# Relative-position bias features computed once per distance, mirrored by TensorE and skewed by the store

## The chip, the cores and the metric

The kernel runs on one core of one Trainium2 chip. The metric is the device time of one execution in microseconds. The kernel before takes 676.85 us, the median of three runs (676.49 to 677.21).

## The reference

Attention with a learned relative-position bias (4 batches, 8 heads, 576 positions, head size 64), followed by a two-layer network on the 2304 tokens. Cut to what matters here:

```
pos = np.arange(S)                                   # S = 576
rel = (pos[:, None] - pos[None, :]).astype(np.float32)
psi_rel = np.log1p(np.abs(rel))
psi_i = np.log1p(np.maximum(pos[:, None], 1.0))
x = (psi_rel / psi_i)[..., None]
h = np.maximum(x @ w1 + b1, 0.0)                     # 32 hidden units
bias = h @ w2                                        # one value per head
scores = scale * q @ k.T + bias.transpose(2, 0, 1)   # then softmax, then @ v
...
h = x @ w_in; r = np.maximum(h, 0.0); g = s * (r * r) + b; out = g @ w_out
```

`psi_i` depends on the row alone and is positive, so `relu(w1*L/psi_i + b1)` is `max(w1*L, -b1*psi_i) / psi_i` up to an added constant, with `L = log1p(|i-j|)`. For one row, everything that depends on the column is a function of `|i-j|`.

## The kernel before, in words

The program writes every engine's order by hand (`tc.manual_schedule()`), so the order of the calls in the source is the order on each engine and on the DMA queue of SyncE (SP). It has three parts.

The bias part builds `bias_d` in DRAM, 8 heads x 576 rows x 576 columns, in 36 steps of 16 rows. The 128 partitions are 4 rows x 32 hidden units; a step has four features, `c` = 0 to 3, one for each group of four rows. A feature `f` (`feature`, L114) is `max(ls, thr)` over 576 columns: `ls` holds `w1*log1p(|g + (S-4) - u|)` for the four rows g of the partitions and 1148 offsets u, and a feature reads the 576 of them that belong to its rows. It is made by VectorE (L121), GpSimd (L123) or ScalarE (L125, as a Relu with another constant, `kc` column 1). Which engine makes which feature stands in the strings of L119 (`vvpa`, `vppa`, `vpvp` in turn) and `ends` (L112). `f` is written as 9 blocks of 64 with a pitch of 68.

`bias_step` (L131) multiplies the four features by the block matrix `w2bd` on TensorE, four 32-column groups of the array side by side, 512 columns (L140) and then 64 (L143), in fp32. A PSUM tile `bps` of one step is emptied by one ScalarE instruction (L147) into `stg`, 128 partitions (16 rows x 8 heads) x 576. One DMA on SP stores it (L153). There are 16 buffers of `f` (four steps) and 10 of `stg`. Features are issued two steps ahead of their matmuls (L619). The last four steps also copy head 0 into `be` of the first pair (`first_head`, L156), and the stores of steps 32 to 34 are held back until step 35.

The attention part works on 16 pairs (a head and two batches), five units of 128 rows each, in the calls `scores`, `biased`, `expo`, `probs_t` and `av`; `bt` holds the bias of rows 0 to 511 of a head and `be` that of its last 64 rows, both read from `bias_d`. GpSimd splits q and k into two parts (`split_qk`, L199 and L200). The first score units stand in `plan` (L605) behind bias steps 33 and 34; the loads of `bt` for the first pair stand behind steps 11, 17, 26 and 33. The network part follows, the last 60% of the time.

Of the kernel before, what the change touches and what calls it, by code (L numbers as in the profile page):

```python
# [26 lines left out]
def attention_moe(ctx, tc, q, k, v, w_in, w_out, dist, par, out):  # L27
# [6 lines left out]
    HALF = S // 2  # L34
    NU = dist.shape[1]
    STEPS = S // 16
# [24 lines left out]

    bias_d = dram.tile([H, S, S], F32, name="bias")
    rs_d = [dram.tile([2, S], F32, name=f"rs{p}") for p in range(NP)]
# [8 lines left out]
    warm = const.tile([128, 1], F32, name="warm")  # L72
    dst = dp.tile([128, NU], F32, name="dst")
    pt_ = dp.tile([128, par.shape[1]], F32, name="pt_")
# [5 lines left out]
    w2x = dp.tile([128, 4, 4 * H], F32, name="w2x")  # L80
    ls = dp.tile([128, NU], F32, name="ls")
    thr = dp.tile([128, 4 * STEPS], F32, name="thr")
# [3 lines left out]
    def setup():  # L86
        hi = S - 64
        nc.sync.dma_start(out=pt_, in_=par)
        nc.scalar.dma_start(out=dst[:, hi:], in_=dist[:, hi:])
        nc.sync.dma_start(out=dst[:, 0:hi], in_=dist[:, 0:hi])  # L90
        nc.vector.memset(warm, 0.0)
        nc.scalar.activation(warm, warm, AF.Exp)
        make_identity(nc, ident)
        wps = ps_t.tile([128, 512], F32, tag="t", name="wps")
        for _ in range(8):
            nc.tensor.matmul(wps[:, 0:128], ident, ident, start=True, stop=True)
        nc.vector.tensor_scalar(thr, li, b1c, -1.0, op0=ALU.mult, op1=ALU.mult)
        nc.vector.tensor_copy(w2x, w2bd.unsqueeze(1).broadcast_to([128, 4, 4 * H]))
        nc.vector.tensor_scalar(off, li, b1c, None, op0=ALU.mult)
        nc.vector.tensor_scalar(ls[:, hi:], dst[:, hi:], w1c, None, op0=ALU.mult)  # L100
        nc.scalar.activation(ls[:, 0:hi], dst[:, 0:hi], AF.Copy, scale=w1c)

# [8 lines left out]
    feats, late = {}, []  # L111
    ends = {STEPS - 4: "vvvp", STEPS - 3: "vvva", STEPS - 2: "vpva", STEPS - 1: "vpva"}  # L112

    def feature(st, c):  # L114
        w = NU - S - 16 * st - 4 * c
        f = fp.tile([128, S // 64, 68], F32, tag="f", name="f")[:, :, 0:64]
        src = ls[:, w:w + S].rearrange("p (a b) -> p a b", b=64)
        col = slice(4 * st + c, 4 * st + c + 1)
        kind = (ends.get(st) or ("vvpa", "vppa", "vpvp")[st % 3])[c]  # L119
        if kind == "v":  # L120
            nc.vector.tensor_scalar(f, src, thr[:, col], None, op0=ALU.max)  # L121
        elif kind == "p":
            nc.gpsimd.tensor_scalar(f, src, FLT_MAX, thr[:, col], op0=ALU.min, op1=ALU.max)  # L123
        else:
            nc.scalar.activation(f, src, AF.Relu, bias=off[:, col])  # L125
        return f, kind == "a"

    def bias_features(st):
        feats[st] = [feature(st, c) for c in (2, 0, 3, 1)]

    def bias_step(st):  # L131
# [6 lines left out]
        pb = ps.rearrange("p a b -> p (a b)")  # L138
        for c in range(4):
            nc.tensor.matmul(  # L140
                pb[32 * c:32 * c + 32, 0:512], w2bd, fs[c][0][:, 0:8], start=True, stop=True)
        for c in range(4):
            nc.tensor.matmul(  # L143
                pb[32 * c:32 * c + 32, 512:S], w2bd, fs[c][0][:, 8:9], start=True, stop=True)
        kcol = kc[:, 1:2] if fs[3][1] else kc[:, 0:1]
        stg = fp.tile([128, S], F32, tag="stg", name="stg", bufs=10)
        nc.scalar.activation(stg, pb[:, 0:S], AF.Identity, scale=nr[:, st:st + 1], bias=kcol)  # L147
        if st >= STEPS - 4:
            first_head(st, stg)
        late.append((st, stg))  # L150
        if st < STEPS - 4 or st == STEPS - 1:
            for i, t in late:
                nc.sync.dma_start(out=bias_d[:, 16 * i:16 * i + 16, :].rearrange("h r j -> r h j"), in_=t)  # L153
            late.clear()

    def first_head(st, stg):  # L156
        r0 = 16 * st % 64
        for x in range(2):
            nc.sync.dma_start(out=bes[0][64 * x + r0:64 * x + r0 + 16, :], in_=stg[0:128:H, :])

# [3 lines left out]
    def load_bias(p, t0, t1):  # L164
# [3 lines left out]
        bt = bts[p]  # L168
        rows = bias_d[h, 128 * t0:128 * t1, :].rearrange("(t p) j -> p t j", p=128)
        nc.sync.dma_start(out=bt[:, t0:t1, 64:], in_=rows)  # L170
        nc.sync.dma_start(out=bt[:, t0:t1, 0:64], in_=rows[:, :, 512:S])

    def load_be(p):
        if p == 0:
            bes[0] = io.tile([128, S], F32, tag="be", name="be", bufs=2)
        elif p < NP and pairs[p][0] == pairs[p - 1][0]:
            bes[p] = bes[p - 1]
        elif p < NP:
            bes[p] = io.tile([128, S], F32, tag="be", name="be", bufs=2)
            for x in range(2):  # L180
                nc.sync.dma_start(out=bes[p][64 * x:64 * x + 64, :], in_=bias_d[pairs[p][0], 512:S, :])

# [411 lines left out]
    def fill():  # L594
# [13 lines left out]
        17: ((load_bias, 0, 1, 2),),  # L608
        20: ((load_v, 0), (load_be, 0)),
        28: ((split_qk, 0, 0),),  # L610
# [165 lines left out]
```

## Time and profile before

| | us |
|---|---|
| three runs, median | 676.85 |
| the profiled execution's own time | 676.67 |
| its span, first to last instruction | 674.5 |
| PE busy in the span | 660.2 (98%) |
| VectorE, ScalarE, GpSimd busy | 449.7, 353.5, 181.2 |

PE is TensorE's matmuls, DVE is VectorE, ACT is ScalarE, POOL is GpSimd, SP is SyncE; a `q` behind an engine's name is its queue, which issues DMAs. The granted clock of TensorE is 1.00 in all slices of the page. A share of busy time over the whole span says little here, because the parts have different limits: it has to be read by stage.

### The profile page before, as it was taken

To read this page: it belongs to the slowest core of one execution; us is meant where nothing else is said; L and a number is where in the kernel's file an instruction comes from. 1 tells how busy PE (TensorE), PEld (TensorE's weight loads), DVE (VectorE), ACT (ScalarE), POOL (GpSimd) and SP (SyncE) were. 2 spreads that over 40 slices of the span, in tenths; PEclk is the share of its full clock that TensorE was granted. 3 is DMA by queue.
4 is the path that set the end of the run, shared out by engine and by line. 5 is a ranking of instruction groups with operands and counts; after the bars stand their busy time and mean duration, and the time that the engine had idled before them with its cause. 6 is when DMAs were issued, how large, how long until landed. Compare 5 with 4: busy or idle time off the path is not lost.

```text
span 674.5 us, 13622 instructions
## 1 busy us (share of the span) xinstructions
PE 660.2 (98%) x5202; PEld 506.4 (75%) x5202; DVE 449.7 (67%) x883; ACT 353.5 (52%) x741; POOL 181.2 (27%) x190
## 2 busy tenths in 40 slices
PE   8997999999999999999999999999999999999997
PEld 4445666776677766688888888888888888888886
DVE  7997898898999877458665356655365754443243
ACT  6997877787777777345543333332333322222221
POOL 7995243453354320012121012220022210000000
PEclk9999999999999999999999999999999999999999
DMA  5997676665766452497628345217335223323312
GB/s 159 285 297 238 193 239 212 206 205 181 239 200 204 145 186 67 122 325 262 214 99 311 127 160 196 81 32 262 128 141 187 64 83 150 121 85 141 109 62 94
DMA packets 53648, 114.84 MB, mean 170 GB/s; under 512 B 10576, under 2 KB 18000, under 8 KB 53584
## 3 DMA queue, kind: packets, MB, share of 16 engines
q1 hardware_dynamic: 53440, 113.65, 50.6%
q8 instruction: 41, 0.67, 0.4%
q10 hardware_dynamic: 144, 0.33, 0.2%
q14 instruction: 23, 0.19, 0.1%
HBM read 84.09 MB, written 29.56 MB: 168 GB/s over the span
## 4 chain that ended last, share of the span: by engine, by line
PE 90%; POOL 3%; DVE 2%; ACT 2%; issue 1%; DMA 1%; SPq 0%; POOLq 0%; DVEq 0%; ACTq 0%
PE hps L472 29%; PE o L497 29%; PE xps L355 10%; PE sps L224 10%; PE tps L288 7%; POOL f L123 3%; PE xps L358 3%; PE bps L140 2%; ACT pr L249 1%; DVE tt L238 1%; DMA pt__123<-in_par_dram 1%; DVE f L121 0%; PE xps L288 0%; DMA bias<-stg 0%; ACT stg L147 0%
## 5 line engine op out<-in xcount | busy, mean ns | idle before, releaser
L497 PE MATMUL o<-wh,gt 128*128 128x512 f32 x576 | 190.3, 390 | 0.0
L472 PE MATMUL hps<-x,wh 128*128 128x512 f32 (+1 forms) x640 | 181.7, 368 | 0.0
L476 ACT ACTIVATE r<-hps 128x512 f32<-128x512 f32 (+1 forms) x80 | 44.5, 556 | 211.5 <-PE hps L472 208.5
L477 DVE SCALAR_TENSOR_TENSOR r<-r,sb 128x512 f32<-128x512 f32 (+1 forms) x80 | 56.9, 711 | 144.2 <-ACT r L476 144.1
L249 ACT ACTIVATE pr<-tt,mn 128x576 f32<-128x576 f32 x144 | 110.9, 771 | 46.5 <-DVE mn L238 45.7
L472 PEld LDWEIGHTS hps<-x,wh 128*128 128x128 f32 x640 | 116.9, 188 | 22.0 <-ACT x L452 0.4
L497 PEld LDWEIGHTS o<-wh,gt 128*128 128x128 f32 x576 | 108.2, 188 | 22.6 <-issue 0.3
L472 PE MATMUL hps<-x,wl 128*128 128x512 f32 (+1 forms) x320 | 117.7, 368 | 0.0
L497 PE MATMUL o<-wl,gt 128*128 128x512 f32 x288 | 112.3, 390 | 0.0
L238 DVE CUSTOM_DVE_ANT_0 tt<-sps,bt 128x576 f32<-128x576 f32 x128 | 91.2, 750 | 7.6 <-PE sps L224 6.0
L224 PE MATMUL sps<-kr,qr 64*128 64x288 f32 (+1 forms) x864 | 87.1, 307 | 1.2 <-ACT stg L147 0.9
L482 DVE SCALAR_TENSOR_TENSOR gt<-r,sb,gt 128x512 fp32r<-128x512 f32 (+1 forms) x80 | 62.6, 783 | 38.3 <-ACT gt L481 38.3
L422 POOL TENSOR_TENSOR wl<-full,wh 128x512 fp32r<-128x512 f32 x32 | 43.3, 1354 | 163.7 <-ACT wh L417 137.9
L481 ACT ACTIVATE gt<-r,sb 128x512 fp32r<-128x512 f32 (+1 forms) x80 | 54.5, 681 | 46.9 <-DVE r L477 46.8
L355 PE MATMUL xps<-pt,vt 128*64 128x288 f32 x512 | 76.0, 419 | 1.7 <-DVE rb L363 0.9
L224 PEld LDWEIGHTS sps<-kr,qr 64*128 64x128 f32 (+1 forms) x864 | 69.2, 186 | 3.5 <-ACT stg L147 1.1
L288 PEld LDWEIGHTS tps<-ident,pr 64*128 64x128 f32 x1216 | 43.9, 137 | 35.5 <-issue 28.4
L472 PEld LDWEIGHTS hps<-x,wl 128*128 128x128 f32 x320 | 60.3, 188 | 10.0
L398 POOL TENSOR_SCALAR full<-full 128x512 f32<-128x512 f32 x32 | 23.8, 742 | 152.4 <-ACT full L396 152.2
L497 PEld LDWEIGHTS o<-wl,gt 128*128 128x128 f32 x288 | 54.1, 188 | 10.4
L288 PE MATMUL tps<-ident,pr 64*128 64x64 f32 x1216 | 55.5, 229 | 2.4 <-ACT pt L319 2.1
L321 DVE COPY pt<-tps 128x512 f32<-128x512 f32 x64 | 43.9, 686 | 12.4 <-PE tps L288 12.3
(66 smaller groups left out, 698.4 us busy)
## 6 DMA issues: line engine op xcount, KB each, us to landing
x<-xs SPq DMA_DIRECT2D x48, 512.0 KB
bias<-stg SPq DMA_DIRECT2D x36, 288.0 KB
raw<-in_moe_w_in_dram SPq DMA_DIRECT2D x16, 512.0 KB
raw<-in_moe_w_out_dram SPq DMA_DIRECT2D x16, 512.0 KB
xs<-x SPq DMA_DIRECT2D x16, 512.0 KB
bt<-bias SPq DMA_DIRECT2D x7, 1152.0 KB
qt<-in_q_dram SPq DMA_DIRECT2D x16, 320.0 KB
kt<-in_k_dram SPq DMA_DIRECT2D x16, 320.0 KB
```

Source lines behind the costliest of these rows:

```text
L224: nc.tensor.matmul(o, a, b, start=(i == 0), stop=(i == 2))
L238: nc.vector.tensor_tensor_reduce(tt.rearrange("p (a b) -> p a b", a=2), ps[x][:, :, 0:HALF], bias.rearrange("p (a b) -> p a b", a=2), -1.0 ...
L249: nc.scalar.activation(pr[:, x], tts.pop((n, x)), AF.Exp, bias=mn[:, x:x + 1], scale=-1.0, accum_out=sums[p][:, col // 3, col % 3:col % 3 ...
L288: nc.tensor.matmul(outs[r], src[d], ident[d, d], is_transpose=True, start=start, stop=True, skip_group_check=not start)
L321: nc.vector.tensor_copy(o, i)
L355: nc.tensor.matmul(ps[64 * x:64 * x + 64, hf, 0:HALF], vt[:, 4 * x + kb, :], pt[:, kb, x, c], start=(kb == 0), stop=False)
L472: nc.tensor.matmul(ps[:, 0:n], w[0, g][:, a, fc], xs_t[s, a][:, j, 0:n], start=(i == 0), stop=(i == 3 * KB - 1))
L476: nc.scalar.activation(r, ps[:, 0:n], AF.Relu)
L477: nc.vector.scalar_tensor_tensor(r, r, sb[:, 0:1], r, op0=ALU.mult, op1=ALU.mult)
L481: nc.scalar.activation(hi, r, AF.Identity, bias=sb[:, 1:2])
L482: nc.vector.scalar_tensor_tensor(lo, r, sb[:, 1:2], hi.bitcast(F32), op0=ALU.add, op1=ALU.subtract)
L497: nc.tensor.matmul(o, gt[:, a, tok], w[1, g][:, fo], start=(fo == 0 and j == 0), stop=(fo == 3 and j == 2))
```

## The change

Everything about a feature now depends on the distance `|i-j|` alone. The host's table `dist` becomes `log1p` of 0, 1, 2, ... in blocks of 16 with a pitch of 20 floats, the same in every partition. A feature of step `st` covers the distances 0 to `16*nb - 1` with `nb = max(S-16*st, 16*st+16)/16` blocks: 576 at both ends of the run, 304 in the middle. GpSimd and ScalarE read a table `ls` without gaps, already multiplied by `w1`; VectorE reads `dst` with its gaps, multiplies by `w1` and takes the maximum in one instruction, over an odd number of blocks. All write `f` without gaps.

TensorE mirrors: PSUM column `a` of a step stands for distance `|a - m|`, `m = 16*st + 15`, over S + 15 = 591 columns; columns below `m` read the feature backwards (step -1), the others forwards. With the cut at 512 columns, which the kernel before has too, this makes three matmuls for each `c` in place of two. Row r of a step needs the 576 columns that start at 15 - r: the store shifts each row by one column (`skewed`), into rows of pitch 608, and `bt` and `be` are read from column 16 on. The engine of a feature comes from running sums (`busy`) in place of the strings. The last 64 rows of head 0 go through a small table in DRAM, `tail_d`, stored by four DMAs and read back by two (`load_be(0)`).

```diff
     HALF = S // 2
-    NU = dist.shape[1]
+    NG16 = dist.shape[1] // 20
     STEPS = S // 16
...
-    bias_d = dram.tile([H, S, S], F32, name="bias")
+    PITCH = S + 32
+    bias_d = dram.tile([H, S, PITCH], F32, name="bias")
+    tail_d = dram.tile([64, PITCH], F32, name="btail")
     rs_d = [dram.tile([2, S], F32, name=f"rs{p}") for p in range(NP)]
...
     warm = const.tile([128, 1], F32, name="warm")
-    dst = dp.tile([128, NU], F32, name="dst")
+    dst = dp.tile([128, NG16, 20], F32, name="dst")
     pt_ = dp.tile([128, par.shape[1]], F32, name="pt_")
...
     w2x = dp.tile([128, 4, 4 * H], F32, name="w2x")
-    ls = dp.tile([128, NU], F32, name="ls")
+    ls = dp.tile([128, 16 * NG16], F32, name="ls")
     thr = dp.tile([128, 4 * STEPS], F32, name="thr")
...
     def setup():
-        hi = S - 64
+        flat = dst.rearrange("p a b -> p (a b)")
+        hi = 20 * (NG16 // 2)
         nc.sync.dma_start(out=pt_, in_=par)
-        nc.scalar.dma_start(out=dst[:, hi:], in_=dist[:, hi:])
-        nc.sync.dma_start(out=dst[:, 0:hi], in_=dist[:, 0:hi])
+        nc.scalar.dma_start(out=flat[:, 0:hi], in_=dist[:, 0:hi])
+        nc.sync.dma_start(out=flat[:, hi:], in_=dist[:, hi:])
         nc.vector.memset(warm, 0.0)
...
         nc.vector.tensor_scalar(off, li, b1c, None, op0=ALU.mult)
-        nc.vector.tensor_scalar(ls[:, hi:], dst[:, hi:], w1c, None, op0=ALU.mult)
-        nc.scalar.activation(ls[:, 0:hi], dst[:, 0:hi], AF.Copy, scale=w1c)
+        k = NG16 // 2
+        nc.vector.tensor_scalar(ls[:, 0:16 * k], dst[:, 0:k, 0:16], w1c, None, op0=ALU.mult)
+        nc.scalar.activation(ls[:, 16 * k:], dst[:, k:, 0:16], AF.Copy, scale=w1c)
...
     feats, late = {}, []
-    ends = {STEPS - 4: "vvvp", STEPS - 3: "vvva", STEPS - 2: "vpva", STEPS - 1: "vpva"}
+    busy = {"v": 0.0, "p": 0.0, "a": 0.0}
...
     def feature(st, c):
-        w = NU - S - 16 * st - 4 * c
-        f = fp.tile([128, S // 64, 68], F32, tag="f", name="f")[:, :, 0:64]
-        src = ls[:, w:w + S].rearrange("p (a b) -> p a b", b=64)
+        nb = max(S - 16 * st, 16 * st + 16) // 16
+        kind = min("vpa" if c == 3 else "vp", key=lambda e: busy[e])
+        if kind == "v":
+            nb += 1 - nb % 2
+        busy[kind] += 0.2 - 0.05 * (kind == "p") + nb / 60.0
+        f = fp.tile([128, 16 * NG16], F32, tag="f", name="f")
+        o, src = f[:, 0:16 * nb], ls[:, 0:16 * nb]
         col = slice(4 * st + c, 4 * st + c + 1)
-        kind = (ends.get(st) or ("vvpa", "vppa", "vpvp")[st % 3])[c]
         if kind == "v":
-            nc.vector.tensor_scalar(f, src, thr[:, col], None, op0=ALU.max)
+            nc.vector.tensor_scalar(o, dst[:, 0:nb, 0:16], w1c, thr[:, col], op0=ALU.mult, op1=ALU.max)
         elif kind == "p":
-            nc.gpsimd.tensor_scalar(f, src, FLT_MAX, thr[:, col], op0=ALU.min, op1=ALU.max)
+            nc.gpsimd.tensor_scalar(o, src, FLT_MAX, thr[:, col], op0=ALU.min, op1=ALU.max)
         else:
-            nc.scalar.activation(f, src, AF.Relu, bias=off[:, col])
+            nc.scalar.activation(o, src, AF.Relu, bias=off[:, col])
         return f, kind == "a"
...
         feats[st] = [feature(st, c) for c in (2, 0, 3, 1)]
+        busy["a"] += 0.83
+        busy["p"] += 2.3 * (st in (26, 28))
...
         pb = ps.rearrange("p a b -> p (a b)")
-        for c in range(4):
-            nc.tensor.matmul(
-                pb[32 * c:32 * c + 32, 0:512], w2bd, fs[c][0][:, 0:8], start=True, stop=True)
-        for c in range(4):
-            nc.tensor.matmul(
-                pb[32 * c:32 * c + 32, 512:S], w2bd, fs[c][0][:, 8:9], start=True, stop=True)
+        m = 16 * st + 15
+        cuts = sorted((0, m, 512, S + 15))
+        for a, b in zip(cuts, cuts[1:]):
+            for c in range(4):
+                mov = fs[c][0][:, m - a:m - b:-1] if b <= m else fs[c][0][:, a - m:b - m]
+                nc.tensor.matmul(pb[32 * c:32 * c + 32, a:b], w2bd, mov, start=True, stop=True)
         kcol = kc[:, 1:2] if fs[3][1] else kc[:, 0:1]
-        stg = fp.tile([128, S], F32, tag="stg", name="stg", bufs=10)
-        nc.scalar.activation(stg, pb[:, 0:S], AF.Identity, scale=nr[:, st:st + 1], bias=kcol)
+        stg = fp.tile([128, S + 16], F32, tag="stg", name="stg", bufs=10)[:, 0:S + 15]
+        nc.scalar.activation(stg, pb[:, 0:S + 15], AF.Identity, scale=nr[:, st:st + 1], bias=kcol)
         if st >= STEPS - 4:
-            first_head(st, stg)
+            r0 = 16 * st - (S - 64)
+            nc.sync.dma_start(out=skewed(tail_d[r0:r0 + 16, :]), in_=stg[0:128:H, :])
+        if st == STEPS - 1:
+            load_be(0)
         late.append((st, stg))
...
             for i, t in late:
-                nc.sync.dma_start(out=bias_d[:, 16 * i:16 * i + 16, :].rearrange("h r j -> r h j"), in_=t)
+                nc.sync.dma_start(out=skewed(bias_d[:, 16 * i:16 * i + 16, :]), in_=t)
             late.clear()
...
-    def first_head(st, stg):
-        r0 = 16 * st % 64
-        for x in range(2):
-            nc.sync.dma_start(out=bes[0][64 * x + r0:64 * x + r0 + 16, :], in_=stg[0:128:H, :])
+    def skewed(rows):
+        heads = [[S * PITCH, H]] if len(rows.shape) == 3 else []
+        return bass.AP(rows.tensor, rows.offset + 1, [[PITCH + 1, 16]] + heads + [[1, S + 15]])
...
         bt = bts[p]
-        rows = bias_d[h, 128 * t0:128 * t1, :].rearrange("(t p) j -> p t j", p=128)
+        rows = bias_d[h, 128 * t0:128 * t1, 16:16 + S].rearrange("(t p) j -> p t j", p=128)
         nc.sync.dma_start(out=bt[:, t0:t1, 64:], in_=rows)
...
     def load_be(p):
-        if p == 0:
-            bes[0] = io.tile([128, S], F32, tag="be", name="be", bufs=2)
-        elif p < NP and pairs[p][0] == pairs[p - 1][0]:
+        if 0 < p < NP and pairs[p][0] == pairs[p - 1][0]:
             bes[p] = bes[p - 1]
...
             for x in range(2):
-                nc.sync.dma_start(out=bes[p][64 * x:64 * x + 64, :], in_=bias_d[pairs[p][0], 512:S, :])
+                rows = tail_d if p == 0 else bias_d[pairs[p][0], 512:S, :]
+                nc.sync.dma_start(out=bes[p][64 * x:64 * x + 64, :], in_=rows[:, 16:16 + S])
...
         17: ((load_bias, 0, 1, 2),),
-        20: ((load_v, 0), (load_be, 0)),
+        20: ((load_v, 0),),
         28: ((split_qk, 0, 0),),
...
     nb, nh, S, D = q.shape
-    g = np.arange(4)
-    u = np.arange(2 * S - 4)
-    dist = np.log1p(np.abs(g[:, None] + (S - 4) - u[None, :]).astype(np.float32))
+    nblk = S // 16 // 2 * 2 + 1
+    dist = np.zeros((nblk, 20), np.float32)
+    dist[:, 0:16] = np.log1p(np.arange(16 * nblk, dtype=np.float32)).reshape(nblk, 16)
     logi = np.log1p(np.maximum(np.arange(S, dtype=np.float32), 1.0)).astype(np.float32)
...
         arrays[n] = np.ascontiguousarray(inputs[n]).view(np.int64)
-    arrays['dist'] = np.repeat(dist.astype(np.float32), hid, axis=0)
+    arrays['dist'] = np.repeat(dist.reshape(1, -1), 4 * hid, axis=0)
     arrays['par'] = par
```

How the instructions move, from the two programs as built (counts behind an `x` are equal neighbours).

GpSimd around the splits of the first pair's q and k (`qr`, `kr`), up to the splits of the second pair. Before:

```order
L123 TENSOR_SCALAR f<-ls,thr 128x9x64 x51
L199 TENSOR_SCALAR qr<-qt 128x640
L200 TENSOR_TENSOR qr<-qt,qr 128x640
L123 TENSOR_SCALAR f<-ls,thr 128x9x64 x3
L199 TENSOR_SCALAR kr<-kt 128x640
L200 TENSOR_TENSOR kr<-kt,kr 128x640
L123 TENSOR_SCALAR f<-ls,thr 128x9x64 x2
L199 TENSOR_SCALAR qr<-qt 128x640
```

After, the same place:

```order
L130 TENSOR_SCALAR f<-ls,thr 128x496 x2
L209 TENSOR_SCALAR qr<-qt 128x640
L210 TENSOR_TENSOR qr<-qt,qr 128x640
L130 TENSOR_SCALAR f<-ls,thr 128x512
L130 TENSOR_SCALAR f<-ls,thr 128x528 x2
L209 TENSOR_SCALAR kr<-kt 128x640
L210 TENSOR_TENSOR kr<-kt,kr 128x640
L130 TENSOR_SCALAR f<-ls,thr 128x544 x2
L130 TENSOR_SCALAR f<-ls,thr 128x560
L130 TENSOR_SCALAR f<-ls,thr 128x576 x3
L209 TENSOR_SCALAR qr<-qt 128x640
```

GpSimd has 63 features now (56 before), of 304 to 576 columns, 27440 in all; of these 59 (25152 columns) belong to steps 0 to 33. Six stand behind the split of `kr`, two before.

TensorE at the first two steps (`bps` is the PSUM tile of a step). Before:

```order
L105 MATMUL cps<-pt__123,w2x 128x1
L140 MATMUL bps<-f,pt__123 32x512 x4
L143 MATMUL bps<-f,pt__123 32x64 x4
L140 MATMUL bps<-f,pt__123 32x512 x4
L143 MATMUL bps<-f,pt__123 32x64 x4
```

After, the same two steps:

```order
L109 MATMUL cps<-pt__124,w2x 128x1
L153 MATMUL bps<-f,pt__124 32x15 x4
L153 MATMUL bps<-f,pt__124 32x497 x4
L153 MATMUL bps<-f,pt__124 32x79 x4
L153 MATMUL bps<-f,pt__124 32x31 x4
L153 MATMUL bps<-f,pt__124 32x481 x4
L153 MATMUL bps<-f,pt__124 32x79 x4
```

A step has 12 matmuls over 591 columns in place of 8 over 576; the trace shows each fp32 matmul as two, so 24 and 16.

SP behind step 31's store, up to the first weight loads (`raw`). Before:

```order
L159 DMA be<-stg 16x576 x4
L170 DMA bt<-bias 128x576
L171 DMA bt<-bias 128x64
L187 DMA qt<-in_q_dram 128x640
L193 DMA kt<-in_k_dram 128x640
L207 DMA vt<-in_v_dram 128x640
L159 DMA be<-stg 16x576 x4
L153 DMA bias<-stg 16x8x576 x4
L384 DMA raw<-in_moe_w_in_dram 128x1024 x2
```

After, the same place (`btail` is `tail_d`):

```order
L159 DMA btail<-stg 16x591 x2
L181 DMA bt<-bias 128x576
L182 DMA bt<-bias 128x64
L197 DMA qt<-in_q_dram 128x640
L203 DMA kt<-in_k_dram 128x640
L217 DMA vt<-in_v_dram 128x640
L159 DMA btail<-stg 16x591 x2
L191 DMA be<-btail 64x576 x2
L165 DMA bias<-stg 16x8x591 x4
L394 DMA raw<-in_moe_w_in_dram 128x1024 x2
```

Eight copies of `be` from SBUF become four stores to DRAM and two loads; the loads read what the stores wrote, and the four held-back stores of the bias stand behind them in the queue.

## Rows read from the trace of the kernel before

**Rows 1.** Busy time by stage: stretch and length; engines' busy us (instructions); clock, DMA, GB/s

```profile
10.00:50.00 40.00, 38.31 (x512) 17.46 (x512) 40.00 (x56) 38.38 (x54) 39.47 (x53) 1.00 0.90 274
50.00:70.00 20.00, 15.68 (x225) 11.54 (x221) 15.46 (x40) 15.94 (x38) 10.10 (x10) 1.00 0.83 257
70.00:270.00 200.00, 199.17 (x2565) 140.48 (x2561) 173.95 (x457) 155.88 (x408) 74.66 (x68) 1.00 0.60 187
```

**Rows 2.** Groups by line and shape, 0 to 85 us: busy, mean ns | idle before

```profile
L121 DVE TENSOR_SCALAR f<-ls,thr 128x576 f32<-128x576 f32 x63 | 45.5, 793 | 0.0
...
L123 POOL TENSOR_SCALAR f<-ls,thr 128x576 f32<-128x576 f32 x56 | 40.3, 748 | 4.5 <-DVE ls L100 4.3
L147 ACT ACTIVATE stg<-bps,kc,pt__123 128x576 f32<-128x576 f32 x36 | 29.7, 826 | 3.3 <-PE bps L143 1.9 <-ACT f L125 1.0 <-ACT pr L249 0.4
L125 ACT ACTIVATE f<-ls,off 128x576 f32<-128x576 f32 x25 | 19.1, 766 | 0.0
...
L100 DVE TENSOR_SCALAR ls<-dst,pt__123 128x636 f32<-128x636 f32 x1 | 0.5, 545 | 0.0
```

**Rows 3.** Timeline, 28.5 to 33 us, VectorE, GpSimd, ScalarE: start us, us, instruction, count

```profile
27.89 5.83 DVE L121 TENSOR_SCALAR f<-ls,thr 128x576 f32<-128x576 f32 x8
...
27.88 5.79 POOL L123 TENSOR_SCALAR f<-ls,thr 128x576 f32<-128x576 f32 x8
...
27.90 0.77 ACT L125 ACTIVATE f<-ls,off 128x576 f32<-128x576 f32 x1
28.57 0.83 ACT L147 ACTIVATE stg<-bps,kc,pt__123 128x576 f32<-128x576 f32 x1
29.28 0.77 ACT L125 ACTIVATE f<-ls,off 128x576 f32<-128x576 f32 x1
```

**Rows 4.** Timeline of TensorE, 28 to 29.4 us, one step and the next's start

```profile
28.11 1.07 PE L140 MATMUL bps<-f,pt__123 128*32 128x512 f32 x8
28.97 0.32 PE L143 MATMUL bps<-f,pt__123 128*32 128x64 f32 x8
29.08 0.59 PE L140 MATMUL bps<-f,pt__123 128*32 128x512 f32 x1
```

**Rows 5.** GpSimd's other sizes, 80 to 100 us; then its timeline, 42 to 51 us

```profile
L199 POOL TENSOR_SCALAR kr<-kt 128x640 fp32r<-128x640 f32 x2 | 1.4, 724 | 0.0
...
L398 POOL TENSOR_SCALAR full<-full 128x512 f32<-128x512 f32 x1 | 0.6, 614 | 3.8 <-ACT full L396 3.8
...
47.11 0.72 POOL L199 TENSOR_SCALAR kr<-kt 128x640 fp32r<-128x640 f32 x1
47.92 1.56 POOL L200 TENSOR_TENSOR kr<-kt,kr 128x640 fp32r<-128x640 f32 x1
49.57 1.46 POOL L123 TENSOR_SCALAR f<-ls,thr 128x576 f32<-128x576 f32 x2
```

**Rows 6.** The chain that ended last, 49 to 53 us: start, us, what

```profile
50.55 0.73 ACT stg L147
51.28 0.04 issue
51.32 0.95 PE sps L224 x10
```

**Rows 7.** DMA of 10 to 50 us; then SP's waits, 5 to 44 us (total, times, longest)

```profile
DMA packets 5646, 10.97 MB, mean 274 GB/s; under 512 B 1003, under 2 KB 1003, under 8 KB 5639
...
q1 hardware_dynamic: 5639, 10.88, 88.8%
...
SPq L170 <- DMA bias<-stg: 3.3, 4, 1.0
```

**Rows 8.** Around `be`: timelines of ScalarE, VectorE and SP, with the chain's DMA row

```profile
56.79 0.83 ACT L147 ACTIVATE stg<-bps,kc,pt__123 128x576 f32<-128x576 f32 x1 [0.36 <-ACT pr L249]
...
58.81 2.74 DMA bias<-stg
...
63.16 0.76 DVE L238 CUSTOM_DVE_ANT_0 tt<-sps,be 128x576 f32<-128x576 f32 x1 [0.25 <-issue]
...
82.28 0.25 SPq L271 DMA_DIRECT2D rs<-rt  x1
...
83.03 1.09 SPq L276 DMA_DIRECT2D rb<-rs  x2
```

## The prediction

> **What bounds the kernel now.** I read the busy times by stage first. From 70 us on TensorE is busy 199.17 of 200 us, and the change has no instruction there: what is gained or lost before moves the end one for one. From 10 to 50 us, in the bias part, VectorE is busy all of the time, GpSimd 39.47 and ScalarE 38.38 of 40 us; TensorE shows 38.31, but that counts matmuls that wait in the pipe. From 50 to 70 us nothing is full [rows 1]. Next the groups by line, for counts and lengths [rows 2], and the timeline, for the pace: eight VectorE features in 5.83 us are (5.83 - 0.79)/7 = 0.72 us from start to start, and GpSimd's the same [rows 3]. ScalarE's take 0.67 (27.90 to 28.57) and one `stg` 0.71 (to 29.28). The strings give VectorE and GpSimd five features each in three steps, 3 x 1.2 us = 3.6 us: three engines are balanced at 1.2 us a step. TensorE needs 0.97 for a step that it doesn't wait in (28.11 to 29.08) [rows 4]. Last the chain: `stg` of step 33 ends at 51.28 and the first scores start at 51.32 [rows 6]. So the end of step 33 sets the start of the attention part, and the sum is made for steps 0 to 33.
>
> **The change part by part.** *GpSimd.* Before: 54 features of steps 0 to 33 at 0.72 us and two splits at 2.46 us (47.11 to 49.57), 38.9 + 4.9 = 43.8 us. For shorter features I take the slope from GpSimd's other sizes: 724 ns at 640 columns, 614 at 512, so 0.86 ns a column [rows 5]; of the 0.72 us at 576 columns 0.495 scale and 0.225 stay. After: 59 x 0.225 + 25152 x 0.86 ns = 13.3 + 21.6, and the splits: 39.8 us, 4.0 less. Between the ends: if all of the 0.72 us scaled, because the gaps of `f` cost the rest, 25152 x 1.25 ns + 4.9 = 36.3 us, and if nothing scaled, 59 x 0.72 + 4.9 = 47.4 us. I take 39.8, because two sizes on this engine give the slope.
>
> *VectorE.* 59 features become 60 with 26432 columns. All scaling: 33.0 us; with 0.2 us that stay, 60 x 0.2 + 26432 x 0.9 ns = 35.8 us. Either way it is below GpSimd's 39.8, which covers it, with 0.065 us to spare for each feature, in case a second pointer scalar or the gaps on the reading side cost something. Without that cover each 0.1 us more on a feature would cost 6 us in all, less 4.
>
> *ScalarE.* 23 features become 17, at most 17 x 0.67 = 11.4, and 34 `stg` of 0.71 with 15 more columns (0.02 each) are 24.8: 36.2 us, covered too.
>
> *TensorE.* 0.97 x 591/576 = 0.995 us a step, 33.8 us. The third piece is below 64 columns in a dozen steps; the 64-column piece of before takes 0.11 us (28.97 to 29.08), so this adds at most 1.3 us. Reading backwards stands nowhere in this trace: I take it at the forward rate, since it is the same column stream, with half speed as the other end (a rival below) and no reason for a gain. In steps 11 to 25, where features are shortest, TensorE has 14.9 us and GpSimd 15.4, so there the two wait for each other: nothing if 16 `f` buffers decouple them, 15 x 0.21 = 3.2 us if each step waits out the drain by which the 1.07 us of a matmul group exceed the 0.86 to its next group. I allow 1.0 us, a chosen value nearer to the low end because the ring is four steps deep.
>
> *Stores.* 88.8% of 40 us on 16 DMA engines, 568 us, went to some 4640 long rows (5639 packets less 1003 small ones) [rows 7]: 0.1225 us a row, 0.98 us a store on each engine (8 rows), 30.4 us for 31 stores, and 5.1 us for loads. For 34 steps that is 38.4 us in 40.8; after, with 2364 bytes for 2304, 39.3 us in some 38. The lag of 1.3 us is hidden by ten `stg` buffers, 11 us deep; SP waited only 3.3 us in four waits for such a store to land. If that cover goes, each us of lag costs one.
>
> *Start and end.* `ls` is made in two halves of 288 and 304 columns in place of 636 and 512. That saves VectorE some 0.25 us, but GpSimd now needs both halves: nothing. Four GpSimd features stand behind those of step 33 in place of two, 2.9 us, and `stg` of step 35 comes 6.2 us after that of step 33 (56.79 against 50.55) [rows 6, 8]: hidden.
>
> *`be` through DRAM.* Before, eight copies landed directly. Now the two loads wait on SP for the last tail store to land, and behind them stand the four held-back stores and the weight loads, whose readers come after 70 us. From the end of `stg` 35 (57.62) to the first use (63.16) are 5.54 us [rows 8]. The new path: one issue 0.55 (half of 1.09), landing, two issues 1.09, landing. A small store landed within 0.75 us (82.28 to 83.03), a large one in 2.74: 3.1 to 7.1 us in sum, so a stall of 0 to 1.6 us. The middle, 5.1, is hidden; I put 0.2.
>
> Sum: -4.0 + 1.0 + 0.2 = -2.8 us against the profiled execution's 676.67 (span 674.5 and 2.2 around it), 673.9. The median of the runs stands 0.2 above that execution: 674.1 us.
>
> **Rivals.** *A: the gain is eaten* (chance 0.20). Not GpSimd but its alternation with TensorE decides (2 us and more of the 3.2), and the round trip of `be` stalls VectorE by up to 1.6 in a stretch where everything hangs on it: about 676.3 us. For it: 14.9 against 15.4. Against: TensorE waits little in the trace although it shares its features with three engines.
>
> *B: TensorE becomes the bound* (0.12), slower than before. A step has 24 matmuls in the trace's count in place of 16. If each costs what it costs in the 0.97 us step, 0.061 us, a step is 1.46 us, 49.6 us for 34, 5.8 more than GpSimd's 43.8 of before: 682.8 us with the stall. Half speed for backward columns, about half of 591, gives the same 1.46. It decides from 43.8/34/24 = 0.054 us a matmul. For it: no stage in the rows runs denser than 512 in 40 us or 2565 in 200. Against: nine matmuls start within 28.97 to 29.08, 0.014 us apart [rows 4], and 0.97 is matched by columns as well.
> [...]
>
> *C: the skewed rows are slow to write* (0.07). Rows now start at any multiple of 4 bytes. With 1.5 times the time of a row, 34 x 1.51 + 5.1 = 56.4 us against 38: 18.4 of lag, 11 of them taken by the ring, 7.4 over: 681.5 us. It decides from 1.37 times. For it: the DMA share of 0.90 leaves no room. Against: nothing in the rows shows an odd start costing anything, nor that it is free.
> [...]
>
> *D: VectorE shuts GpSimd out* (0.04). `ls` with 636 columns took 545 ns where a feature of 576 took 793 [rows 2]: VectorE has a faster form. If the features ran in it and kept GpSimd off meanwhile, 26432 x 545/636 ns = 22.6 us would add to the 39.8: 62.4 against 43.8, 692.7 us. Against: the features of before, 9 blocks written from a flat source, stayed in the slow form; now an odd number of blocks is read and a flat row written.
> [...]
>
> **How the numbers follow.** The forecast, the stage shorter by GpSimd's saving less what its partners take back, has 0.57, with its own range of 670.6 (all of 0.72 scaling, then ScalarE's 36.2 and 0.5 of friction bind) to 675.4. A has 0.20, B 0.12, C 0.07, D 0.04. The range for 8 in 10 leaves out D, half of B and C, and a little below: 670.6 to 682.0. A measurement of this kernel can tell 0.2%, 1.35 us, from no change. Faster by more: 0.58 (forecast and the edge of A); within: 0.19; slower: 0.23.
>
> **What would show it.** Right: GpSimd's features 0.72 us apart at 576 columns and 0.49 at 304; VectorE's below 0.75 us apart at the ends and not bunched between GpSimd's; a TensorE step near 1.0 us in the middle; `stg` of step 33 ending near 48.3; the part from 70 us on as long as before, 2.8 us earlier. Wrong: TensorE steps of 1.4 us with VectorE and GpSimd idle (B); `stg` waiting for DMA (C); GpSimd features of 1 us (D); a wait of over 1 us for `be` at its first use (A).

## The result, and the profile after

The changed kernel takes 680.61 us, the median of six runs (678.91 to 681.58), beside 676.86 us before (six runs, 676.49 to 677.21): ratio 1.0053, 95% interval 1.0039 to 1.0068, slower by 3.75 us. Forecast were 674.1 us. The profiled execution took 680.71 us with a span of 678.7, 4.2 us more than before.

By stage, in the columns of [rows 1], with the stretches of 60 to 80 us apart:

```profile
10.00:50.00 40.00, 37.45 (x780) 27.07 (x776) 37.10 (x61) 33.62 (x49) 38.53 (x62) 1.00 0.89 273
50.00:70.00 20.00, 13.30 (x191) 10.47 (x185) 11.01 (x30) 12.87 (x30) 7.98 (x7) 0.81 0.70 209
70.00:270.00 200.00, 199.57 (x2549) 141.15 (x2547) 173.12 (x454) 155.25 (x406) 74.24 (x68) 0.99 0.61 195
...
60.00:65.00 5.00, 1.08 (x17) 0.72 (x17) 0.00 (x0) 0.72 (x3) 4.48 (x4) 0.73 0.47 131
65.00:70.00 5.00, 4.09 (x34) 3.48 (x36) 4.09 (x13) 3.36 (x9) 0.00 (x0) 0.50 0.90 266
70.00:75.00 5.00, 4.93 (x41) 3.68 (x39) 3.20 (x8) 3.04 (x11) 0.00 (x0) 0.50 0.98 367
75.00:80.00 5.00, 5.00 (x68) 3.27 (x65) 2.92 (x8) 3.26 (x9) 0.00 (x0) 0.91 0.45 135
```

In 60 to 65 us VectorE does nothing and TensorE next to nothing; in the ten microseconds behind it TensorE is busy, but at a granted clock of 0.50. The chain that ended last shows what stood there (start, us, what; steps under 0.1 us left out):

```profile
47.31 0.85 ACT stg L156
48.20 0.95 PE sps L234 x8
...
57.45 4.12 DMA btail<-stg
61.62 0.48 SPq L191
62.15 2.70 DMA be<-btail
65.08 0.76 DVE tt L248
...
73.93 2.12 PE xps L365 x8
76.04 0.65 PE tps L298 x16
```

The bias part became shorter, as forecast: `stg` of step 33 ends at 48.16 where it ended at 51.28 [rows 6], 3.1 us earlier. Then VectorE's first use of `be` waits for the last tail store and the load behind it. Without that wait it would start at 60.1 (the unit before it starts its last sum at 58.49, and in a run below without the wait `be` follows 1.60 us after that); it starts at 65.08, a stall of 5.0 us. From there to the second pair's first turn (`tps`, TensorE's transposes of the probabilities) are 10.96 us (76.04); before, 8.43 (63.16 in [rows 8], to the row below). That is 2.5 us of work at the lower clock. The chain of the kernel before, its step that answers to 76.04:

```profile
71.59 0.64 PE tps L288 x16
```

Sum: -3.1 + 5.0 + 2.5 = +4.4, against +4.2 of the span.

Why the tails land so late is read on SP's queue (start, us for the issues, instruction, count). After:

```profile
46.07 3.98 SPq L165 DMA_DIRECT2D bias<-stg  x5
50.17 2.20 SPq L159 DMA_DIRECT2D btail<-stg  x2
54.60 0.32 SPq L181 DMA_DIRECT2D bt<-bias  x1
...
55.45 0.42 SPq L197 DMA_DIRECT2D qt<-in_q_dram  x1
...
56.39 0.43 SPq L217 DMA_DIRECT2D vt<-in_v_dram  x1
56.87 1.11 SPq L159 DMA_DIRECT2D btail<-stg  x2
61.62 1.12 SPq L191 DMA_DIRECT2D be<-btail  x2
```

Before, the load of `bt` for unit 3 in the same place:

```profile
52.88 1.16 SPq L170 DMA_DIRECT2D bt<-bias  x1
```

This load waits for the store of step 31 to land. The `stg` that it stores, on ScalarE before and after:

```profile
47.67 0.83 ACT L147 ACTIVATE stg<-bps,kc,pt__123 128x576 f32<-128x576 f32 x1 [1.00 <-ACT f L125]
...
43.18 0.84 ACT L156 ACTIVATE stg<-bps,kc,pt__124 128x591 f32<-128x591 f32 x1
```

It ends 4.5 us earlier now (44.02 for 48.50), but its store lands 1.7 us later: by the landing records of the traces at 54.52 for 52.77, each just ahead of the load's issue. That is 10.5 us behind the end of the `stg` in place of 4.3; for 5.2 of the 10.5 us the store, the last of the five at 46.07, waits on SP to be issued (49.18). Behind the load of `bt` SP issues 960 KB of q, k and v and only then the last two tails; the later of them was ready when `stg` of step 35 ended (54.59). In the packet records (one for each row: 32 of 2364 bytes for these two tails) the tails' rows of 2364 bytes run from 59.8 to 61.1, among the last of the loads' rows of 2560 bytes (to 60.9): they queued in the DMA engines behind the loads. Before, the same loads' rows ended at 60.4, so this part of the stream did not move. From the end of `stg` 35 to the first use of `be` are 10.5 us (54.59 to 65.08).

Features and emptying by shape (as [rows 2], 0 to 85 us):

```profile
L156 ACT ACTIVATE stg<-bps,kc,pt__124 128x591 f32<-128x591 f32 x36 | 29.9, 841 | 6.5 <-PE bps L153 5.3 <-ACT pr L259 0.4
...
L130 POOL TENSOR_SCALAR f<-ls,thr 128x576 f32<-128x576 f32 x5 | 3.6, 744 | 3.6 <-ACT ls L105 3.6
...
L130 POOL TENSOR_SCALAR f<-ls,thr 128x304 f32<-128x304 f32 x4 | 2.0, 551 | 0.0
L130 POOL TENSOR_SCALAR f<-ls,thr 128x496 f32<-128x496 f32 x3 | 2.0, 678 | 0.8 <-PE bps L153 0.8
...
L128 DVE TENSOR_SCALAR f<-dst,pt__124,thr 128x592 f32<-128x592 f32 x2 | 1.8, 882 | 0.0
...
L128 DVE TENSOR_SCALAR f<-dst,pt__124,thr 128x304 f32<-128x304 f32 x3 | 1.6, 575 | 0.0
```

### The profile page after: what moved, and what is told of

Read it like the earlier page. It is cut to its first block, busy times and chain, and to the rows that moved or that the text cites. A ratio compares the mean times of both kernels' runs of the same rounds, so it can differ in the third digit from the quotient of the medians.

```text
span 678.7 us, 14207 instructions
## 1 busy us (share of the span) xinstructions
PE 660.8 (97%) x5490; PEld 518.1 (76%) x5490; DVE 444.4 (65%) x883; ACT 348.1 (51%) x734; POOL 179.0 (26%) x197
## 4 chain that ended last, share of the span: by engine, by line
PE 92%; DVE 2%; ACT 1%; DMA 1%; issue 1%; POOL 1%; SPq 0%; DVEq 0%; POOLq 0%; ACTq 0%
PE hps L482 29%; PE o L507 29%; PE sps L234 10%; PE xps L365 10%; PE tps L298 7%; PE bps L153 4%; PE xps L368 3%; DVE f L128 1%; ACT pr L259 1%; DMA btail<-stg 1%; POOL f L130 1%; DVE tt L248 1%; DMA pt__124<-in_par_dram 0%; PE xps L298 0%; DMA be<-btail 0%
## 5 line engine op out<-in xcount | busy, mean ns | idle before, releaser
L234 PE MATMUL sps<-kr,qr 64*128 64x288 f32 (+1 forms) x864 | 89.8, 313 | 5.0 <-DVE mn L248 4.3
L234 PEld LDWEIGHTS sps<-kr,qr 64*128 64x128 f32 (+1 forms) x864 | 71.3, 191 | 7.5 <-DVE mn L248 5.4
L507 PEld LDWEIGHTS o<-wl,gt 128*128 128x128 f32 x288 | 54.1, 188 | 10.5
```

What stands on the lines that cost most here:

```text
L234: nc.tensor.matmul(o, a, b, start=(i == 0), stop=(i == 2))
L507: nc.tensor.matmul(o, gt[:, a, tok], w[1, g][:, fo], start=(fo == 0 and j == 0), stop=(fo == 3 and j == 2))
```

## The experiments

**The wait for `be` taken away.**

```diff
-        if st == STEPS - 1:
-            load_be(0)
...
-                rows = tail_d if p == 0 else bias_d[pairs[p][0], 512:S, :]
+                rows = bias_d[0, 0:64, :] if p == 0 else bias_d[pairs[p][0], 512:S, :]
...
-        20: ((load_v, 0),),
+        20: ((load_v, 0), (load_be, 0)),
```

> The changed kernel with be of the first pair read at step 20 from rows 0 to 63 of head 0, which landed long before (so one tile holds other rows of the bias); the tail stores still run, nobody reads them. The wait for be is gone with everything else in place. If the stall and the clock after it are the whole loss (5.0 and 2.5 us in the trace): 680.6 - 7.5 = 673.1 us, clock 1.00 throughout. If part of the loss lies elsewhere (mirrored matmuls, skewed rows, extra traffic): above 675 us.

Measured: 675.46 us (673.66 to 677.61, eleven runs), ratio 0.9982 (0.9971 to 0.9993); the profiled execution took 673.66 with the clock at 1.00. So everything but the wait makes the kernel faster: against the changed kernel's ratio of 1.0053 the wait and its clock are worth 0.7%, 4.8 us in the median and 7 between the two profiled executions. The profiled execution is the fastest of the eleven. The median lies above 675, where the expectation has part of the loss elsewhere: the runs spread over 4 us, and a run below shows that the wait of `bt` for store 31 has a part in that.

**The loads.** First those ahead of the tails are moved behind the held-back stores:

```diff
-        33: ((load_bias, 0, 3, 4), (load_q, 2), (load_k, 2), (load_v, 1), (scores, 0), (biased, 0, 0), (expo, 0, 0), (biased, 0, 1), (expo, 0, 1)),
+        33: ((load_bias, 0, 3, 4), (scores, 0), (biased, 0, 0), (expo, 0, 0), (biased, 0, 1), (expo, 0, 1)),
...
-        35: ((load_w, *early[0]), (load_w, *early[1])),
+        35: ((load_q, 2), (load_k, 2), (load_v, 1), (load_w, *early[0]), (load_w, *early[1])),
```

> The changed kernel with the loads of q and k of the third pair and v of the second moved on SP from ahead of the last two tail stores to behind the held-back stores. Theory Q (the last tail stores wait in the DMA engines behind 0.96 MB of these loads, and the loads of be wait for them): tail stores issued at 55.5 instead of 56.9 land by 57.5 instead of 61.6, be lands by 60 to 61, the 5.0 us stall of VectorE shrinks below 1, TensorE's granted clock stays at 1.00: 673.2 to 674.5 us. Rival S (storing a tail and reading it back is itself slow, about 4.1 and 2.7 us whatever stands ahead): be lands near 63.5, stall 3.5, some clock lost: 678 to 680 us.

Then, with and without that, the second pair's q and k and the first pair's v are moved to the start:

```diff
     load_k(0)
+    load_q(1)
+    load_k(1)
+    load_v(0)
     bias_features(0)
...
-        6: ((load_q, 1), (load_k, 1)),
-        20: ((load_v, 0),),
```

Both moves:

> The run with the loads behind (third pair's q and k, second's v), and besides the loads of q and k of the second pair and v of the first moved to the start of the program, where the DMA engines idle from 6 to 9 us. Theory L (the store stream is what lags: it fills the DMA engines to the end of the bias part, store 31 lands no earlier than before the change, and what waits for it on SP, bt of unit 3, the tails and be, becomes the end of the path; how late varies from run to run): 0.96 MB less in the stream lands store 31 some 3 us earlier, near 51, nothing waits for bt or be any more, all runs lie within 1 us of 673.5. Rival V (the scatter of 673.8 to 678.8 us comes from something else, such as the clock by itself): median near 676 with the same scatter.

This one alone:

> The changed kernel with only the second pair's q and k and the first pair's v loaded at the start; the loads ahead of the last tail stores stay where they are. Theory L: SP is free from about 51.5 instead of 54.6, the last two tails are issued as soon as step 35 is done (54.6) and land behind the rest of the 0.96 MB by 57.5 to 58.5, be by 60.5 to 61.5: a stall of 0.5 to 1.5 us in place of 5.0, clock near 1.00, 673.5 to 675.5 us. If only the loads ahead of the tails matter (theory Q alone): 679 to 680.6 us.

Measured: moved behind, 676.66 us (673.78 to 678.78, twelve runs; ratio 0.9993, 0.9980 to 1.0006); moved to the start, 675.24 (673.23 to 677.28, twelve; 0.9976, 0.9964 to 0.9988); both 673.81 (673.09 to 674.29, five; 0.9954, 0.9942 to 0.9966). Each move alone brings back most of the loss but leaves a spread of 4 to 5 us; together they bring all of it, and the spread falls to 1.2. So theory Q alone was not enough: its 673.2 to 674.5 us was met by the profiled execution (674.15, near the fast end of its runs), not by the median. Theory L's ranges hold for both runs that it was made for, and rival S, a round trip that is slow by itself, is refuted. SP's queue with both moves:

```profile
48.98 0.33 SPq L181 DMA_DIRECT2D bt<-bias  x1
...
52.24 2.74 SPq L159 DMA_DIRECT2D btail<-stg  x2
56.33 1.12 SPq L191 DMA_DIRECT2D be<-btail  x2
```

and VectorE's first use of `be` in it (idle time ahead in brackets):

```profile
58.37 0.75 DVE L248 CUSTOM_DVE_ANT_0 tt<-sps,bt 128x576 f32<-128x576 f32 x1
...
59.97 0.76 DVE L248 CUSTOM_DVE_ANT_0 tt<-sps,be 128x576 f32<-128x576 f32 x1 [0.24 <-PE sps L234]
```

Store 31 lands by 48.98 instead of 54.60, and `be` waits for the scores alone. The stage was not shortened by it (`stg` 33 ends at 48.04), so the loads had held up the stores and not the engines.

The same in the kernel before, the early loads alone and both moves:

> The kernel before with only the second pair's q and k and the first pair's v loaded at the start. There VectorE, GpSimd and ScalarE bound the bias part and bt and be land before they are needed, so a shorter store stream brings nothing: 676.7 us. If the store stream holds up the kernel before as well: 1 to 3 us less.

> The kernel before with both moves of loads (second pair's q and k and first pair's v to the start; third pair's q and k and second's v behind the held-back stores). Control for the run with both moves in the changed kernel, 673.8: if that gain is the change's shorter bias part and not the loads', the kernel before stays at 676.7 us; if the loads alone bring it, 674 us.

Measured: 676.63 us (ratio 0.9996, 0.9988 to 1.0005) and 676.54 (1.0002, 0.9993 to 1.0011). The moves bring nothing where the bias part is 3 us longer: the 3 us gained with them are the change's own.

**The round trip alone, in the kernel before.**

```diff
+    tail_d = dram.tile([64, S], F32, name="btail")
...
-            first_head(st, stg)
+            r0 = 16 * st - (S - 64)
+            nc.sync.dma_start(out=tail_d[r0:r0 + 16, :], in_=stg[0:128:H, :])
+        if st == STEPS - 1:
+            load_be(0)
...
-                nc.sync.dma_start(out=bes[p][64 * x:64 * x + 64, :], in_=bias_d[pairs[p][0], 512:S, :])
+                nc.sync.dma_start(out=bes[p][64 * x:64 * x + 64, :], in_=tail_d if p == 0 else bias_d[pairs[p][0], 512:S, :])
```

> The kernel before with the last 64 rows of head 0 stored to a table in DRAM by four DMAs and read back by two, in place of eight direct copies; nothing else is changed (rows unskewed, features and matmuls of before). Theory Q: the last tail store is issued at 57.6 behind the same loads, lands near 61, be near 64.5: a stall of 1 to 2 us and some time at the lower clock, 678 to 680 us. If the round trip hurts only together with the skewed rows or the longer stores: 676.9 us.

Measured: 676.82 us (ratio 1.0003, 0.9994 to 1.0011), clock 1.00: no change. That is the time of the second expectation, though not by its reason, since unskewed and shorter stores cure nothing in the changed kernel (below); theory Q had put too much on the loads alone. Its chain (steps under 0.1 us left out):

```profile
57.80 2.41 DMA btail<-stg
60.26 0.48 SPq L178
60.79 2.80 DMA be<-btail
63.82 0.76 DVE tt L235
```

The tail lands in 2.41 us, not 4.12, and VectorE idles 0.76 us ahead of `be`, where it idles 0.25 before [rows 8]. Storing and reading back is cheap where the stage ends late; it became dear where the stage ended 3 us earlier and the work of the DMA engines did not.

**How the stall divides.** `bt` of unit 3 read from rows that landed long before (`r0 = 0 if (p, t0) == (0, 3) else 128 * t0`), in the changed kernel and in the run without the wait for `be`:

> The changed kernel with only bt of unit 3 read from rows that landed long before; be goes through DRAM as in the changed kernel and waits for its tails. SP is no longer held to 54.6 us, the loads of q, k and v are issued some 3 us earlier, and the last tails as soon as step 35 is done, near 54.6. If SP's hold-up is half of the stall: tails land by 58 to 59.5 behind the loads, be by 61 to 62.5, a stall of 1 to 2.5 us and little lost clock, 674.5 to 677 us. If the loads ahead of the tails are all of it: stall near 5 us, 680 us.

> The run without a wait for be, and besides bt of unit 3 of the first pair read from rows 0 to 127, which landed long before (so unit 3 of the first pairs gets other rows of the bias). Neither of the two loads waits for the store stream any more, all traffic stays. If the scatter left without the wait for be (673.7 to 677.6 us) is bt's wait for store 31: all runs within 1 us of 673.5, clock at 0.999 or 1.00. If the scatter has another source: again about 4 us wide.

Measured: 678.56 us (674.17 to 679.60, eight runs; ratio 1.0020, 1.0003 to 1.0038) and 674.84 (673.64 to 675.53, six; 0.9973, 0.9961 to 0.9984). In the first, SP issues the last tails at 55.62 instead of 56.87, but they still take 4.04 us to land:

```profile
55.62 1.11 SPq L159 DMA_DIRECT2D btail<-stg  x2
60.28 1.12 SPq L192 DMA_DIRECT2D be<-btail  x2
```

`be` is used at 64.24, so `bt`'s wait is 0.8 of the 5.0 us in this execution; most of the rest is what stands ahead of the tails in the DMA engines, stores and loads. Neither expectation came out: the stall is 4.2 us, and the loads of q, k and v are issued 1.2 us earlier (54.21 for 55.45), not 3, since SP still issues everything ahead of them. The parts don't simply add: one of the eight runs took 674.17 us at a clock of 1.00, like a run without a stall. In the second run the spread fell from 4.0 to 1.9 us, where 1 us to either side of 673.5 was expected: `bt`'s wait accounts for part of it; the rest, and why the median stays 1.0 us above the run with both moves, stays open.

**TensorE's clock.** 20 matmuls (`ident` by `ident`) in `step` at `n == 3`, ahead of the scores of unit 5:

> The changed kernel with 20 extra fp32 matmuls of 128 columns (about 4.3 us) put on TensorE just where it idles for be, into PSUM columns that nobody reads. The stall stays. If the granted clock fell because TensorE idled, and that cost the 2.5 us: the clock stays at 1.00 from 60 to 80 us and the time is 678.1 us. If the clock has nothing to do with it, or the part after is slow for another reason: 680.6 us or more, the stretch from the first use of be to the turn of the next pair still near 10.9 us.

Measured: 686.61 us (684.68 to 690.83; ratio 1.0156, 1.0133 to 1.0179). They did not run in the gap: their PSUM tile is read by a ScalarE copy that itself stands behind the wait for `be`. They ran behind it, at the lower clock (0.82 in the mean of 50 to 70 us, 0.84 in that of 70 to 90), 40 records in 7.51 us:

```profile
67.01 7.51 PE xps L543 x40
74.52 1.04 PE sps L234 x11
```

This tells nothing on the cause. The second try put them into the free columns of the scores' own tile:

```diff
+        if n == 5:
+            for _ in range(20):
+                nc.tensor.matmul(ps[0][:, 0, 384:512], ident, ident, start=True, stop=True)
```

> The changed kernel with 20 extra fp32 matmuls of 128 columns (3.8 us at the higher clock) in front of the scores of unit 5, into columns of their own PSUM tile that nobody reads; that tile is free at 61.2 us, so they run while VectorE waits for be. The stall stays near 5 us. If idling is what lowers the granted clock: clock 1.00 to 80 us, the stretch from the first use of be to the second pair's first turn back at 8.4 us, 678.1 us. If not: 680.6 us or more.

Measured: 679.00 us (678.16 to 679.83; ratio 1.0032, 1.0020 to 1.0044), in the profiled execution (678.66) with the clock at 1.00 throughout:

```profile
62.17 4.66 PE sps L235 x40
66.83 1.03 PE sps L237 x11
...
73.99 0.64 PE tps L301 x16
```

`be` is used at 65.63 there, after about the same stall (VectorE idles 5.08 us ahead of it, 5.2 in the changed kernel), and the second pair's turn comes 8.36 us later in place of 10.96: the 2.6 us are the clock's, and the clock fell because TensorE idled. The time gained less: 2.05 us between the profiled executions, since `be` was used 0.55 us later here (the unit ahead of it came 0.7 later), and 1.6 in the median; the two slowest of the five runs have a mean clock of 0.995 and 0.997, so in them it fell for a time all the same.

**Suspects cleared.** Stores not skewed (`[[PITCH, 16]] + heads + [[1, S]]`), and all pieces read forwards (`fs[c][0][:, 0:b - a]`):

> The changed kernel with its stores (the bias and the tails) not skewed: 576 columns per row, every row at the same column of the same pitch of 608 (so the mirrored rows are shifted wrongly, the values of the bias are others). Theory L with the stream bound by its bytes: 2304 for 2364 bytes per row is 2.5%, 0.8 us of the stream to store 31; the stall for be stays above 3 us: 679 to 680.6 us. Rival C (odd starts make the rows slow): store 31 lands 2 us or more earlier, the stall falls below 2.5 us: 674 to 677 us. In the packet records a skewed row took 95 ns (median) and a row of 2304 bytes 93, which speaks against C.

> The changed kernel with all pieces read forwards (step 1 in place of -1; the columns below the diagonal get the values of other distances). If reading with step -1 runs at the forward rate: a step of TensorE in the middle stays at 1.07 us, the end of stg 33 at 48.2, 680.6 us. If reading backwards is slower, the middle is shorter by up to half of a step's columns and step 33 ends earlier.

Measured: 679.96 us (ratio 1.0050, 1.0038 to 1.0063) and 679.81 (1.0046, 1.0034 to 1.0058). Unskewed, `bt` waits to 54.45 and `be` to 65.16, as skewed; the bias part ended 1.2 us later in this execution (49.37), so VectorE idles 4.1 us for `be` and not 5.2, still above the 3 expected. Forwards, `stg` of step 33 ends at 48.14, as backwards. Neither has a visible part in the loss; the pitch of 608 columns was the same in all of these runs and was not tried by itself.

**More buffers**, with both moves of loads: `fp` with `bufs=24` for 16.

> The changed kernel with both moves of loads and 24 buffers for f in place of 16, so that VectorE and GpSimd may run six steps ahead of TensorE in place of four. If the alternation of GpSimd and TensorE (TensorE's chain in the middle, the features after 36 us) costs what the prediction allowed as friction, 1.0 us comes back: 672.8 us. If the engines don't wait for each other there: 673.8 us.

Measured: 672.57 us (672.21 to 672.85; ratio 0.9939, 0.9927 to 0.9951). `stg` of step 33 ends at 47.34, 0.7 us earlier, and GpSimd is busy for 39.30 of the 40 us from 10 to 50 (38.59 with both moves and 16 buffers). By the ratios 1.0 us came back, as expected. This beats both kernels: the one before took 676.42 in the same runs, 3.9 us more.

## Why the prediction was wrong

*The stage came out as put, in part by luck.* It became 3.1 us shorter where -4.0 and +1.0 of friction were put, and ended at 48.16 where "near 48.3" stood. Its terms are others. GpSimd takes 744 ns for 576 columns and 551 for 304, 0.71 ns a column where 0.86 was taken: its sum is then 41.1 us (59 x 0.31 + 25152 x 0.71 ns + 4.9), 2.7 less than before and not 4.0. The friction was real, one wait for TensorE of 0.8 us (the row of 496 columns above); with 24 buffers the stage ends 0.7 us earlier. And the start, put at nothing, gave 0.7: GpSimd's first feature starts at 4.88 in place of 5.61. These make 2.6 of the 3.1 us; the rest stays open.

*TensorE (rival B) and the mirrored reading.* The emptying of three steps in the middle, by ScalarE's timeline, takes the time from 22.12 to 25.11:

```profile
22.12 2.80 ACT L156 ACTIVATE stg<-bps,kc,pt__124 128x591 f32<-128x591 f32 x3
25.11 0.84 ACT L156 ACTIVATE stg<-bps,kc,pt__124 128x591 f32<-128x591 f32 x1 [0.18 <-PE bps L153]
```

A step is 1.00 us, as put (0.995), and 24 matmuls in it are 0.042 us each, below the 0.054 from which B decides.

*Skewed rows (rival C).* In the packet records a skewed row of 2364 bytes takes 95 ns (median), one of 2304 bytes 93 in the kernel before: 1.02, no more than its bytes (1.03). *D*: VectorE takes 882 ns for 592 columns, near the pace of the features before (793 for 576) and not that of `ls` (545 for 636), and GpSimd is not shut out: 744 ns for 576 columns, 748 before.

*The step that failed* is "`be` through DRAM", put at 0.2 us with a stall of 0 to 1.6. The window was judged rightly: 5.5 us from the end of `stg` 35 to the first use without a wait (54.59 to 60.1), as before. The path was summed as 3.1 to 7.1 us from landings of 0.75 to 2.74 us; it took 10.5: SP issued the first of the last two tails 2.3 us after both were ready and the second 0.6 later, that one landed in 4.12 us, and the issue and landing of the load behind it added 3.5. A nearer price than the 0.75 us stood in the trace of before: by its landing records the last direct copy of `be`, issued at 58.18 behind the same loads, landed at 61.76, 3.6 us later.

The delay goes back to the sentence on the stores: "The lag of 1.3 us is hidden by ten `stg` buffers". Store 31 came to lie 10.5 us behind its `stg` and not 4.3, 6.2 more where 1.3 were put. The ring hid the lag from ScalarE (from 5 to 50 us it waited for TensorE and VectorE alone), and the stage did get shorter. It did not hide it from what stands behind the stores on SP and waits for them to land. The DMA engines were busy for 0.89 of the time from 10 to 50 us, as before; a stage 3 us shorter left their stream where it was, so the loads and tails queued behind it came later, seen from the end of the stage, by at least the stage's own gain. Why store 31 landed even 1.7 us later than before is not shown; unskewed rows of 2304 bytes landed as late (`bt` at 54.45), though in an execution whose stage ended 1.2 us later, so the longer rows may have a part in it. The landings of `be` were judged with the old stream; the round trip alone fits that one, as the run in the kernel before shows. Rival A named the place (a round trip that stalls VectorE), with a third of its size. That TensorE loses its clock after such a stall, 2.5 us more, stood in no term. The prediction's own sign for a miss, a wait of over 1 us at the first use of `be`, is what the trace shows. The time lies inside the range of 670.6 to 682.0 us only because half of B and C was counted into it, and neither of them happened.

Two sums of the prediction don't come out, without bearing on the miss: D's 692.7 counts GpSimd's saving twice (674.1 + 22.6 are 696.7), and the low end of the forecast's range adds up to 670.1 (676.9 - 7.5 + 0.5 + 0.2), not 670.6.

## What to carry to other kernels

When a stage gets shorter, ask of every queue that runs beside it whether its stream gets shorter too; where it does not, as here, each wait behind it moves by the whole gain (3.1 us) towards the end of the path. Take the price of a transfer from one in the same place of the queue, not from a quiet stretch (3.6 us and 0.75 here). A ring of buffers hides a late store from its producer only: look for its readers, and for what else stands behind them in the queue. A stall in front of a TensorE-bound stretch can cost more than its own length (5.0 us of stall cost 2.5 more here), so price the clock with it.

## What was not expected of the hardware

- With 4.3 us without a matmul (to 65.91) TensorE's granted clock showed 0.50 from 65 to 75 us, which cost 2.5 us; with matmuls in the gap it stayed at 1.00 in the profiled execution.
- The pace of the same DMA stream differs between executions: with the same instructions ahead of it, `bt` of unit 3 could be issued at 54.60 in the changed kernel and at 51.47 in the run with loads behind, which moved 291 GB/s from 10 to 50 us where 273 were moved. Each kernel has one profile, and none of a late run of that one exists, so the cause of the spread is not shown.
- Reading a moving operand (the feature that streams through TensorE) in fp32 with step -1 cost nothing that shows: `stg` of step 33 ended at 48.16 with it and at 48.14 without.
